# A spectral filter and a feed-forward on one core: W_in loaded in seven small pieces, the prologue rearranged around it, and stages B and Y a slot later

## Chip, core and metric

One core of one Trainium2 chip runs the whole program. The metric is the device time of one execution in microseconds (us). Each timed execution also lists its span (first to last instruction) and the mean clock that TensorE was granted. "Before" is the kernel as it stood, "changed" the kernel with the change.

## The reference, cut to what matters

```python
# x: (8, 3008, 256) f32; filt_r, filt_i: (1505, 256); w_in: (256, 2048); w_out: (2048, 256)
X = np.fft.rfft(x, axis=1)
y = np.fft.irfft(X * (filt_r + 1j * filt_i)[None], n=3008, axis=1)
h = np.maximum(y.reshape(24064, 256) @ w_in, 0.0)
out = (h * h) @ w_out
```

## The kernel before

The transform of length 3008 = 64 x 47 is done with matmuls, per batch: stage A (47 points) gives u, which goes through DRAM (dU) to be reordered; B (64 points), a product with the filter on VectorE, P back, giving ze, which goes through DRAM (dZ) and comes back as zt; stage Y gives yt, the input of the feed-forward. The feed-forward runs in 47 groups of 512 tokens, each group in 8 slots. In a slot TensorE does four matmuls of 512 columns (psH) and eight of 256 (psO, for the group before), and units of the next batch's stages are sprinkled into chosen slots. Batch 0's stages, and most of batch 1's stage A, form a prologue of some 50 us.

```python
    def load_win(k):                       # W_in, f32, in the same two buffers as x
        w32s[k] = p_x32.tile([128, DFF], F32, tag="x32", ...)
        nc.sync.dma_start(out=w32s[k], in_=moe_w_in[128 * k:128 * k + 128, :])
    ...
    def read_z(b, c, ks=(0, 1)):           # Z back from DRAM, two halves
        for k in ks:
            nc.sync.dma_start(out=zt[64 * k:64 * k + 48],
                              in_=v[48 * k:48 * k + 48, 8 * c:8 * c + 8, :])
    ...
    def fft_plan(b):                       # slot numbers, cut
        t0 = 14 if b == 1 else 18
        for p in range(12):
            r = t0 + (18 if b == 1 else 19) * p // 11
            put(r, 0, unit_b, b, p); put(r, 0, unit_s, b, p); put(r + 2, 1, unit_p, b, p)
        t0 = 35 if b == 1 else 40
        ... read_z at t0 ...
        for n in range(16):
            if b == 1:
                put(38 + n // 2 if n > 3 else 39, n % 2, unit_y, b, n)
            else:
                put(44 + n // 2, n % 2, unit_y, b, n)
    ...
    for k in range(7):                     # prologue: batch 0's B, product, P
        ... unit_b, place_f, unit_p0 ...
        if k in (1, 2):                    # here two of the three x tiles of batch 1 are loaded
            load_wide(1, k - 1)
            cast_wide(1, k - 1, nc.gpsimd, nc.gpsimd)
    read_z(0, 0); load_wout(0); read_z(0, 1); load_wout(1)
    for c in (0, 2, 1):
        chunk_a(1, c)                      # batch 1's stage A, three of four chunks
    for c in (0, 2, 1):
        write_u(1, c)
    for n in range(4):
        unit_y(0, n)                       # then the feed-forward starts
```

## Time and profile before

| what | value |
|---|---|
| timed executions, median (3) | 794.77 us (794.66 to 795.65) |
| the profiled execution's own time | 797.61 us, span 795.8 |
| its mean granted clock | 0.996 |
| TensorE / VectorE / ScalarE busy | 98% / 69% / 70% |
| first feed-forward matmul | 52.5 us from the span's start |

The execution that was profiled took 2.84 us longer than the timed median. The profile is read in the prediction.

### The profile page before, as it was taken

The numbers are of one execution on the slowest core, as the hardware profiler recorded it, in microseconds if no ns is written. First come the engines' busy times: TensorE is split into PE (matmuls) and PEld (weight loads), VectorE is DVE, ScalarE is ACT, GpSimd is POOL, SyncE is SP. The second block draws the span as 40 slices with busy tenths as digits, with TensorE's granted clock in tenths as the row PEclk, the third lists the DMA queues.
The fourth block names the chain that finished last, engine by engine and source line by source line (L and its number), as shares of the span: only waits on it lengthen the run. The fifth ranks groups of instructions, "written<-read, shape, count | busy, mean of one in ns | idle before, by whom it ended". The sixth has DMA issues, their size and how long they took to land.

```text
span 795.8 us, 14801 instructions
## 1 busy us (share of the span) xinstructions
PE 783.1 (98%) x6102; PEld 553.7 (70%) x6102; DVE 552.2 (69%) x898; ACT 554.9 (70%) x708; POOL 24.4 (3%) x27
## 2 busy tenths in 40 slices
PE   8989999999999999999999999999999999999998
PEld 5846677667676676867778676776777667776666
DVE  6946995579855897559965699557985589554342
ACT  3856776767777677767777677676776767766664
POOL 3710000000000000000000000000000000000000
PEclk9989999999999999999999999999999999999999
DMA  9994555336724467055471555525563342511111
GB/s 352 361 277 134 130 151 139 92 126 165 202 58 107 158 165 181 30 164 151 124 183 49 171 153 137 129 71 156 156 170 97 87 142 80 123 48 41 40 41 54
DMA packets 88139, 107.32 MB, mean 135 GB/s; under 512 B 6288, under 2 KB 78864, under 8 KB 83856
## 3 DMA queue, kind: packets, MB, share of 16 engines
q1 hardware_dynamic: 87864, 106.19, 46.9%
q8 instruction: 48, 0.79, 0.4%
q10 hardware_dynamic: 144, 0.18, 0.1%
q14 instruction: 19, 0.16, 0.1%
q0 software_dynamic: 64, 0.00, 0.0%
HBM read 58.12 MB, written 48.23 MB: 134 GB/s over the span
## 4 chain that ended last, share of the span: by engine, by line
PE 93%; DMA 3%; ACT 1%; DVE 1%; issue 0%; POOL 0%; SPq 0%; ACTq 0%; DVEq 0%; POOLq 0%
PE psO L577 40%; PE psH L560 39%; PE psA L359 3%; PE psY L530 3%; PE psB L443 2%; PE psP L494 2%; PE warm L274 1%; DMA ut<-dU 1%; DMA xw<-in_x_dram 1%; PE psf L293 1%; DMA dZ<-ze 1%; ACT h L564 1%; PE psf L296 0%; DMA dU<-u 0%; PE psA L380 0%; ACT sF L303 0%
## 5 line engine op out<-in xcount | busy, mean ns | idle before, releaser
L564 ACT ACTIVATE h<-psH 128x1024 f16<-128x1024 f32 x376 | 385.2, 1025 | 189.7 <-PE psH L560 188.2
L577 PE MATMUL psO<-sWout,h 128*128 128x256 f16 x3008 | 388.6, 272 | 0.0
L560 PE MATMUL psH<-yt,sWin 128*128 128x512 f16 (+7 forms) x1728 | 386.9, 351 | 1.7 <-DVE yt L539 0.8
L577 PEld LDWEIGHTS <-h 128*128 128x128 f16 x3008 | 290.6, 98 | 77.3
L568 DVE TENSOR_TENSOR h<-h 128x1024 f16<-128x1024 f16 x376 | 253.7, 685 | 100.8 <-ACT h L564 99.2
L560 PEld LDWEIGHTS <-sWin 128*128 128x128 f16 x1728 | 159.5, 98 | 101.7 <-issue 3.5
L451 DVE TENSOR_TENSOR prod<-psB,sF 128x1024 f16<-128x1024 f32 x84 | 102.4, 1219 | 5.9 <-PE psB L443 5.6
L539 DVE CAST yt<-psY 128x376 f16<-128x376 f32 x62 | 33.9, 549 | 57.4 <-PE psY L530 57.4
L365 DVE CAST u<-psA 96x512 f16<-96x512 f32 x50 | 34.3, 687 | 47.3 <-PE psA L359 45.1
L496 ACT CAST ze<-psP 128x512 f16<-128x512 f32 x84 | 49.2, 586 | 17.8 <-PE psP L494 15.9
L588 ACT COPY ost<-psO 128x512 f32<-128x512 f32 (+1 forms) x96 | 55.7, 580 | 6.7 <-PE psO L577 5.3
L530 PEld LDWEIGHTS <-zt 112*128 112x128 f16 x512 | 34.9, 98 | 12.1 <-issue 2.0
L530 PE MATMUL psY<-sC,zt 112*128 112x94 f16 x512 | 42.3, 205 | 0.6 <-DMA zt<-dZ 0.3
L465 DVE TENSOR_TENSOR yf<-prod,yf 128x512 f16<-128x512 f16 x84 | 35.7, 425 | 2.9
L443 PE MATMUL psB<-ut,sSB 128*128 128x256 f16 x192 | 36.5, 272 | 0.6 <-DMA ut<-dU 0.5
L359 PE MATMUL psA<-x,sC 94*96 94x512 f16 x96 | 36.6, 382 | 0.0
L443 PEld LDWEIGHTS <-sSB 128*128 128x128 f16 x192 | 18.6, 98 | 20.9 <-issue 1.7
L494 PE MATMUL psP<-yf,sSP 128*128 128x256 f16 x168 | 32.1, 273 | 0.2 <-ACT yt L537 0.2
L537 ACT CAST yt<-psY 128x376 f16<-128x376 f32 x66 | 30.7, 468 | 1.1 <-PE psY L530 0.6
L338 DVE CAST x<-x 94x2048 f16<-94x2048 f32 x24 | 29.2, 1216 | 0.0
L363 ACT CAST u<-psA 96x512 f16<-96x512 f32 x50 | 28.6, 572 | 0.0
L458 DVE COPY yf<-prod 64x512 f16<-64x512 f16 x84 | 24.3, 289 | 2.9
(63 smaller groups left out, 255.9 us busy)
## 6 DMA issues: line engine op xcount, KB each, us to landing
x<-in_x_dram SPq DMA_DIRECT2D x20, 768.0 KB
zt<-dZ SPq DMA_DIRECT2D x64, 192.0 KB
dU<-u SPq DMA_DIRECT2D x28, 384.0 KB
dZ<-ze SPq DMA_DIRECT2D x28, 384.0 KB
out_dram<-ost SPq DMA_DIRECT2D x66, 128.0 KB
out_dram<-ost SPq DMA_DIRECT2D x31, 256.0 KB
ut<-dU SPq DMA_DIRECT2D x7, 1024.0 KB
xw<-in_x_dram SPq DMA_DIRECT2D x4, 1024.0 KB
```

Source lines behind the costliest of these rows:

```text
L359: nc.tensor.matmul(ps[0:96, :], sSA, x16s[(b, c)][:, m, :], start=True, stop=True)
L443: nc.tensor.matmul(ps[:, i * D:(i + 1) * D], sSB[:, 2 * p + i, :], uts[b][:, 2 * p + i, :], start=True, stop=True)
L451: nc.vector.tensor_mul(out=prod, in0=ps.rearrange("p (a d) -> p a d", d=D).unsqueeze(1).to_broadcast([128, 2, 2, D]), in1=sF[:, :, 2 * p:2 ...
L465: nc.vector.tensor_add(out=yf, in0=prod[:, 0], in1=yf)
L494: nc.tensor.matmul(ps[:, i * D:(i + 1) * D], sSP[:, 2 * p + i, :], yf[:, i, :], start=True, stop=True)
L496: nc.scalar.copy(out=zes[(b, c)][:, 2 * i6:2 * i6 + 2, :], in_=ps.rearrange("p (a d) -> p a d", d=D))
L530: nc.tensor.matmul(ps[:, 94 * jj:94 * jj + 94], zt[:, 4 * (g % 2) + jj, dt * 128:(dt + 1) * 128], sSY, start=True, stop=True)
L560: nc.tensor.matmul(ps[:, i, o:o + n], sWin[:, dt, jt * 128:(jt + 1) * 128], yts[b][:, dt, r:r + n], start=(dt == 0), stop=(dt == 1))
L564: nc.scalar.activation(out=h2[:, 2 * s:2 * s + 2, :], in_=ps, func=AF.Relu)
L568: nc.vector.tensor_mul(out=v, in0=v, in1=v)
L577: nc.tensor.matmul(pso[g][:, t % 2, :], h2s[g][:, jt, t * 128:(t + 1) * 128], sWout[:, jt, :], start=(jt == 0), stop=(jt == NJT - 1))
L588: nc.scalar.copy(out=ost[:, h0:h0 + step, :], in_=pso[g][:, h0:h0 + step, :])
```

## The change

Its intent is to get all of x of batch 1 in early (so far one of its three tiles was, the other two waited for W_in's buffers): W_in no longer uses the x buffers but seven pieces in buffers that the main loop needs later. Around that, the filter's casts and evictions are spread differently over the engines. In the main loop B and Y of batches 2 to 7 come one slot later (more time for ut and zt to land), and batch 1's four Y units in one slot are spread out, for which its B is squeezed into one slot less. Cut to its core:

```diff
-    def load_win(k):
-        w32s[k] = p_x32.tile([128, DFF], F32, tag="x32", name=f"win32_{k}")
+        for k, c, n, pool, tag in ((0, 0, 768, p_ze, "ze"), (0, 768, 768, p_ze, "ze"),
+                                   (0, 1536, 512, p_prod, "prod"), ... 7 pieces ...):
+            nc.sync.dma_start(out=t, in_=moe_w_in[128 * k:128 * k + 128, c:c + n])
 ...
-        t0 = 14 if b == 1 else 18
+        t0 = 14 if b == 1 else 19
-            r = t0 + (18 if b == 1 else 19) * p // 11
+            r = t0 + (17 if b == 1 else 18) * p // 11
-        t0 = 35 if b == 1 else 40
+        t0 = 34 if b == 1 else 40
-                put(38 + n // 2 if n > 3 else 39, n % 2, unit_y, b, n)     # b == 1
-                put(44 + n // 2, n % 2, unit_y, b, n)                      # b > 1
+            put((38 if b == 1 else 45) + n // 2, n % 2, unit_y, b, n)
 ...
+    load_win()
+    for k in range(3):
+        load_wide(1, k)                    # x of batch 1, right behind W_in
 ...                                       # filter casts, place_f order: cut
-        if k in (1, 2):
-            load_wide(1, k - 1)
-            cast_wide(1, k - 1, nc.gpsimd, nc.gpsimd)
+    cast_wide(1, 2, nc.vector, nc.scalar)
```

More of the change, by code (lines that the diff above doesn't have):

```diff
@@ L210 @@
     xw32, xw16 = {}, {}
-    halves, later = ((0, 0), (0, 1)), []
     def load_wide(b, k):
@@ L218, in load_wide, with cast, cast_wide @@
         t = pool.tile([128, 8, D], F32, tag=tag, name=f"xw_{b}_{k}")
-        v = (v0[:, 0:8, :], v1, v0[:, 8:16, :])[k]
-        for m in (slice(0, 4), slice(4, 8)) if (b, k) in halves else (slice(0, 8),):
-            if m.stop > 4 and m.start == 4:
-                later.append((t, v, m))
-            else:
-                nc.sync.dma_start(out=t[:, m, :], in_=v[:, m, :])
-        xw32[(b, k)] = t
-    def cast_wide(b, k, *engs, parts=(0, 1)):
-        if 0 in parts:
-            xw16[(b, k)] = p_x16.tile([128, 8, D], F16, tag="x16", name=f"xw16_{b}_{k}")
-        for i in parts:
+        nc.sync.dma_start(out=t, in_=(v0[:, 0:8, :], v1, v0[:, 8:16, :])[k])
+        xw32[(b, k)] = t
+    def cast(eng, out, in_):
+        (eng.copy if eng is nc.scalar else eng.tensor_copy)(out=out, in_=in_)
+    def cast_wide(b, k, *engs):
+        t = p_x16.tile([128, 8, D], F16, tag="x16", name=f"xw16_{b}_{k}")
+        for i in range(2):
             m = slice(4 * i, 4 * i + 4)
-            engs[i].tensor_copy(out=xw16[(b, k)][:, m, :], in_=xw32[(b, k)][:, m, :])
-    for k in range(2):
+            cast(engs[i], t[:, m, :], xw32[(b, k)][:, m, :])
+        xw16[(b, k)] = t
+    for k in range(3):
         load_wide(0, k)
-    for t, v, m in later:
-        nc.sync.dma_start(out=t[:, m, :], in_=v[:, m, :])
-    load_wide(0, 2)
     f32s = []
@@ L276, with place_f @@
     f16s = []
-    def place_f(im, k, eng, rotate=False):
+    def place_f(im, k, *engs, rotate=False):
         if rotate:
@@ L299, in place_f @@
             n = t.shape[1]
+            eng = engs[i % len(engs)]
             dst = sF[:, im, 4 * k + 2 * i:4 * k + 2 * i + 2 * n, :]
@@ L311, with load_win, cast_win @@
     w32s = {}
-    def load_win(k):
-        w32s[k] = p_x32.tile([128, DFF], F32, tag="x32", name=f"win32_{k}")
-        nc.sync.dma_start(out=w32s[k], in_=moe_w_in[128 * k:128 * k + 128, :])
-    def cast_win(k):
-        for j in range(2):
-            c = slice(1024 * j, 1024 * j + 1024)
-            nc.gpsimd.tensor_copy(out=sWin[:, k, c], in_=w32s[k][:, c])
+    def load_win():
+        for k, c, n, pool, tag in ((0, 0, 768, p_ze, "ze"), (0, 768, 768, p_ze, "ze"),
+                                   (0, 1536, 512, p_prod, "prod"), (1, 0, 768, p_ze, "ze"),
+                                   (1, 768, 512, p_prod, "prod"), (1, 1280, 512, p_prod, "prod"),
+                                   (1, 1792, 256, p_yf, "yf")):
+            t = pool.tile([128, n], F32, tag=tag, name=f"win32_{k}_{c}")
+            nc.sync.dma_start(out=t, in_=moe_w_in[128 * k:128 * k + 128, c:c + n])
+            wins.append((t, k, slice(c, c + n)))
+    def cast_win():
+        for t, k, c in wins:
+            nc.gpsimd.tensor_copy(out=sWin[:, k, c], in_=t)
+    wins = []
     def load_wout(k):
@@ L390, in chunk_a, with chunk_a0 @@
                     eng.tensor_copy(out=o, in_=pv)
-    def chunk_a0(c, ks):
-        for k in ks:
+    def chunk_a0(c):
+        for k in range(2):
             banks, groups = bank_pair(f"psA_0_{c}_{k}")
@@ L641, in fft_plan @@
         for n in range(16):
-            if b == 1:
-                put(38 + n // 2 if n > 3 else 39, n % 2, unit_y, b, n)
-            else:
-                put(44 + n // 2, n % 2, unit_y, b, n)
+            put((38 if b == 1 else 45) + n // 2, n % 2, unit_y, b, n)
         return plan
@@ L653 @@
     uT = p_h2.tile([128, 2, NC, 128], F16, tag="h2", name="uT")
-    for i in range(2):
-        for k in range(2):
-            cast_wide(0, k, nc.vector, nc.vector, parts=(i,))
-    cast_wide(0, 2, nc.vector, nc.gpsimd)
+    for k in range(3):
+        cast_wide(0, k, nc.vector, nc.gpsimd if k == 2 else nc.vector)
     def load_const(t, d, k):
@@ L666 @@
         load_const(sSP[:, c, :], dSP, k)
-    for k in range(2):
-        load_win(k)
-    for k in range(2):
-        for c in (0, 2):
-            chunk_a0(c, (k,))
-    for k in range(2):
-        for c in (1, 3):
-            chunk_a0(c, (k,))
+    load_win()
+    for k in range(3):
+        load_wide(1, k)
+    for c in (0, 2, 1, 3):
+        chunk_a0(c)
     f16s.append(p_h2.tile([128, 2, QF + D], F16, tag="h2", name="f16"))
@@ L678 @@
         nc.gpsimd.tensor_copy(out=f16s[0][:, im, QF:], in_=nyq[:, im, :])
-    for im, e in ((0, e0), (0, e1), (1, e0)):
-        nc.gpsimd.tensor_copy(out=f16s[0][:, im, e], in_=f32s[im][:, e])
-    for k in range(2):
-        sSPx.append(p_u.tile([128, 12, 128], F16, tag="u", name=f"sSPx_{k}"))
-        c = slice(12 * k, 12 * k + 12)
-        nc.gpsimd.tensor_copy(out=sSPx[k][0:64], in_=sSP[64:128, c, :])
-        nc.gpsimd.tensor_copy(out=sSPx[k][64:128], in_=sSP[0:64, c, :])
-    for k in range(2):
-        cast_win(k)
-    uts[0] = p_ut.tile([128, NC, D], F16, tag="ut", name="ut_0")
-    load_wide(1, 2)
-    cast_wide(1, 2, nc.gpsimd, nc.gpsimd)
-    for k in range(6):
-        turn_u(k, nc.vector if k in (1, 3, 4, 5) else nc.scalar)
-        if k > 2:
-            place_f(0, k - 3, nc.scalar, True)
-    nc.vector.tensor_copy(out=f16s[0][:, 1, e1], in_=f32s[1][:, e1])
-    place_f(0, 3, nc.vector, True)
-    place_f(1, 0, nc.scalar)
+    for e in (e0, e1):
+        nc.gpsimd.tensor_copy(out=f16s[0][:, 0, e], in_=f32s[0][:, e])
+    uts[0] = p_ut.tile([128, NC, D], F16, tag="ut", name="ut_0")
+    turn_u(0, nc.scalar)
+    turn_u(1, nc.vector)
+    turn_u(2, nc.scalar)
+    turn_u(3, nc.vector)
+    place_f(0, 0, nc.scalar, rotate=True)
+    for eng, e in ((nc.vector, slice(0, 1024)), (nc.gpsimd, slice(1024, 2048)),
+                   (nc.scalar, slice(2048, QF))):
+        cast(eng, f16s[0][:, 1, e], f32s[1][:, e])
+    turn_u(4, nc.vector)
+    place_f(0, 1, nc.scalar, rotate=True)
+    turn_u(5, nc.vector)
+    place_f(1, 0, nc.scalar, nc.vector, rotate=True)
+    for k in range(6):
+        if k % 3 == 0:
+            sSPx.append(p_u.tile([128, 12, 128], F16, tag="u", name=f"sSPx_{k}"))
+        c, o = slice(4 * k, 4 * k + 4), slice(4 * k % 12, 4 * k % 12 + 4)
+        nc.gpsimd.tensor_copy(out=sSPx[-1][0:64, o, :], in_=sSP[64:128, c, :])
+        nc.gpsimd.tensor_copy(out=sSPx[-1][64:128, o, :], in_=sSP[0:64, c, :])
+    cast_win()
+    for k in range(2):
+        cast_wide(1, k, nc.gpsimd, nc.gpsimd)
     for k in range(7):
@@ L705 @@
             unit_p0(k - 1)
-        if k < 2:
-            place_f(0, k + 4, nc.scalar)
-        if k in (1, 2):
-            load_wide(1, k - 1)
-            cast_wide(1, k - 1, nc.gpsimd, nc.gpsimd)
+        if k < 4:
+            place_f(0, k + 2, nc.scalar)
+    cast_wide(1, 2, nc.vector, nc.scalar)
     read_z(0, 0)
```

## The prediction

> **What bounds the kernel now.** I read the page first (busy shares, slices, chain), then each engine's busy time in stretches, then the waits of TensorE and of the DMA queue, and last the timeline of the stretch that the change rebuilds. The page and the stretches:
>
> ```profile
> PE 783.1 (98%) x6102; PEld 553.7 (70%) x6102; DVE 552.2 (69%) x898; ACT 554.9 (70%) x708; POOL 24.4 (3%) x27
> ...
> 24.80:40.70 15.90, 14.85 (x139) 12.56 (x137) 14.08 (x13) 13.70 (x13) 12.91 (x12) 1.00 0.91 340
> 40.70:52.50 11.80, 9.72 (x50) 5.19 (x48) 4.61 (x7) 5.20 (x8) 2.03 (x2) 0.71 0.87 235
> 52.50:63.00 10.50, 9.30 (x51) 4.22 (x51) 7.52 (x13) 8.40 (x10) 0.00 (x0) 1.00 0.96 273
> 63.00:126.00 63.00, 62.79 (x468) 43.62 (x466) 53.47 (x90) 45.22 (x59) 0.00 (x0) 1.00 0.54 147
> 126.00:132.00 6.00, 5.38 (x63) 4.04 (x61) 2.75 (x6) 4.03 (x7) 0.00 (x0) 1.00 0.78 196
> 132.00:796.00 664.00, 659.57 (x5098) 468.54 (x5095) 451.91 (x744) 468.25 (x596) 0.00 (x0) 1.00 0.42 116
> ```
>
> The columns of a stretch are its length, then busy time of PE, PEld, DVE, ACT, POOL, then clock, DMA share and GB/s. From 63 us on TensorE is full, so only its own gaps can be won there. I added up start-to-start distances of all matmuls less their columns at the full rate: after 60 us the gaps come to about 5 us in all, in few places. The loose stretch is 40.7 to 52.5: 9.7 of 11.8 us busy, and at a clock of 0.71. What happens in it, engine by engine:
>
> ```profile
> 38.71 1.01 ACT L482 CAST ze<-psP 128x1024 f16<-128x1024 f32 x1 [0.30 <-PE psP L480]
> 40.85 1.01 ACT L482 CAST ze<-psP 128x1024 f16<-128x1024 f32 x1 [1.13 <-PE psP L480]
> ...
> 41.64 2.03 POOL L232 CAST xw<-xw 128x1024 f16<-128x1024 f32 x2 [2.26 <-DMA xw<-in_x_dram]
> ...
> 40.65 0.38 PE L378 MATMUL psA<-xw,sC 128*96 128x512 f16 x1
> 42.74 0.58 PE L380 MATMUL psA<-xw,sC 120*96 120x512 f16 x1 [1.71 <-POOL xw L232]
> 43.12 0.63 PE L378 MATMUL psA<-xw,sC 128*96 128x512 f16 x1
> 43.54 0.63 PE L380 MATMUL psA<-xw,sC 120*96 120x512 f16 x1
> ```
>
> Batch 1's stage A has started when it waits for the cast of x, which waits for a load issued at 34.44 and landed at 41.5. That load came so late because its buffer held W_in, cast only at 29.9 to 33.9. The second cost is in the last two lines: matmuls of 512 columns start 0.42 us apart, where later ones stand 0.22 apart. The clock record has the half clock from 41.9 to 48.7 us. The DMA queue's waits name what comes next:
>
> ```profile
> SPq L483 <- ACT ze L482: 16.1, 6, 8.8
> ...
> SPq L512 <- DMA dZ<-ze: 3.8, 4, 2.0
> ```
>
> Batch 0's Z goes through DRAM. From the landing records: the last ze is evicted at 41.86, its write lands at 44.59, the read of zt that needs it is issued at 44.60 and lands at 47.79. Stage Y of batch 0 began at 50.65, so this round trip had 2.9 us of slack. It is the next bound. For the main loop, the waits of TensorE after 60 us:
>
> ```profile
> PE psH L560 <- DVE yt L539: 0.8, 2, 0.5
> PE psB L443 <- DMA ut<-dU: 0.5, 1, 0.5
> PE psY L530 <- DMA zt<-dZ: 0.3, 1, 0.3
> PE psY L530 <- ACT yt L537: 0.3, 1, 0.3
> ```
>
> **What the Trainium skill says.** "TensorE: Matmul & The Clock Gate", part 1 on the HAM clock gate: the array falls to half clock after an idle window of about 3.4 us, windows run freely, and it needs a busy window to return. The trace agrees: the half clock lasted 6.83 us, two such windows, after a window (38.4 to 41.9) in which I count 1.3 us of matmuls. The page states no share of busy time at which a window counts as idle; here 1.3 us of 3.41 was too little, and the window from 52.1 with some 2.0 us was enough. "DMA: Bandwidth & Descriptors", section on the anatomy of one DMA, gives a fixed cost of about 2 us and bytes at 436 GB/s (measured there on the GpSimd path). The trace: 256 KB of Z took 2.7 us from issue to landing, 192 KB of zt 3.2 us, and 1 MB loads on a full queue landed 2.5 us apart. "VectorE: DVE Perf Modes", section on the TRN2 errata, says small instructions each pay a fixed latency on VectorE and ScalarE; it does not speak of GpSimd, where the change cuts sSPx into three times as many copies.
>
> **The change part by part.**
> 1. First x loads whole instead of in halves. The halves were cast at 5.8, 8.4, 9.5; whole tiles should land at about 7, 9.5, 12 from the same bytes. The warm-up matmuls end at 10.9 anyway. Worth 0.
> 2. W_in into seven pieces in ze, prod and yf buffers. Bytes are the same 2.1 MB and land by about 30.5, as before. GpSimd casts them at 29.9 to 34, as before (4 x 1.04 us becomes 7 smaller ones, perhaps +0.2). But the x buffers are free from the start: x of batch 1 is queued right behind W_in and lands at about 33.1, 35.6, 38.1 (2.5 us each). GpSimd casts the first two (2 x 2.03 us) from 34.1 to 38.2. Stage A needs them at 40.7: no wait. The third is cast by DVE and ACT after the loop (0.7 and about 1 us) and is needed only by the third chunk.
> 3. Stage A then is 24 x 0.217 = 5.2 us, 40.7 to 45.9, instead of ending at 50.65. This removes 1.9 us of wait and 14 x 0.21 = 2.9 us of half clock, 4.8 us in all.
> 4. The filter's imaginary part is cast by three engines at its landing (21.3) instead of half by GpSimd and the rest by DVE at 23.1. DVE's 1024 columns take 0.7, GpSimd's 1.04, ACT's about 0.95: done at 22.4. ACT then evicts place_f(0,1), 2 x 0.58 us, and place_f(1,0), 1.1 us, to 24.6. (By my count of the bank pairs, the latter falls on a single two-bank tile, so the second engine it names is not used.) First prods at 24.65 instead of 26.19: 1.5 us earlier.
> 5. But place_f(0,2..5) now all lie in the loop on ACT: 15 evictions instead of 13 after place_f(1,0). In the old loop they follow each other every 1.1 us (28.49, 29.63, 30.73, 31.83). place_f(1,5) is the twelfth: 24.6 + 12 x 1.11 = 37.9. Then the last two prods, 2 x 1.17: 40.25, the last P matmuls, and ze at about 40.9, which is where it stood (40.85). Part 4 is spent on part 5: sum 0.
> 6. So Y of batch 0 starts when zt lands, about 41.9 + 2.6 + 3.1 = 47.6, instead of 50.65: **3.0 us won of the 4.8**; the other 1.8 us turn into TensorE idling between 45.9 and 47.6.
> 7. Slots: B and Y of batches 2 to 7 a slot later give ut and zt about 2 us more. Gaps that I counted there: 0.13 at 166, 0.15 at 216, 0.67 at 261, 0.23 at 357, 0.47 at 597, sum 1.65. Batch 1: four Y units in one slot cost 0.43 + 0.21 + 0.47 = 1.1 us at 126.7 to 128.7; two a slot should free most. Against that, its B is squeezed into 17 slots where DVE is full (15.50 of 16 us busy from 76 to 92), and its zt is needed a slot earlier: I take back 0.7 us. Net **2.0 us**.
>
> Sum: 794.8 - 3.0 - 2.0 = 789.8. Nothing follows behind the main loop that could hide it, since TensorE is full to the end.
>
> **Rivals.**
> - *The half clock returns in a new place.* The idle 1.7 us before Y leaves about half of one window busy (0.6 us of A, some 1.1 of Y), between the 1.3 us that throttled and the 2.0 us that did not. If it throttles, some 4 slots of the first feed-forward group run 4 x 0.43 instead of ACT's 1.05 us pace: +2.5 us, about 792.3. I give it 0.35, which adds 0.9 in the mean. Against it: TensorE comes out of 5 dense microseconds.
> - *ACT is the bound of the prologue loop.* It was busy 13.70 of 15.90 us and gets two more evictions in it. If its pace is 1.2 rather than 1.11, ze ends 1 us later and so does Y: 791 without the throttle, 793 with it. If buffers let ACT run at its bare 1.05, ze comes 0.3 earlier.
> - *The Z trip is shorter than I think*, since no x load shares the queue any more: Y at 46.6, 789 or, with a full clock and all slot gaps gone, 788.
> - *Batch 1's denser B stalls TensorE through DVE*: the 2.0 us of part 7 shrink to 0.5. For it: DVE had to do some 39 us of work in a 36.5 us stretch by my sum already. Against: only one gap, 0.38 us at 83, came of it.
>
> **Range and chances.** 789.8 plus 0.9 for the throttle's chance gives 790.8 (rounded up). The ends are the third rival (788.2) and throttle plus slow ACT (793.6). Two per cent would be 15.9 us, more than the about 14 us of gaps after the warm-up, so faster by over 2% is nearly out; slower needs a stall of a size that no part suggests.
>
> **What would show it.** Right: no wait of stage A for x, its matmuls 0.22 apart; x of batch 1 landed before 39; first Y matmul between 46.5 and 48 after a wait for zt; last ze at about 41 with ACT nearly gapless before it; no pair of gaps near 126; no psB wait for ut in batches 2 to 7. Wrong: stage A still at half clock or waiting (GpSimd late), a clock below 1 in the stretch after Y starts, last ze past 42.5, new gaps between 75 and 115 where psP or psB waits for DVE, or seven small W_in loads that hold up the queue so that x lands after 40.

## The result, and the profile after

| | before | changed |
|---|---|---|
| median of the timed executions (4 each) | 795.21 us (794.66 to 796.75) | 793.79 us (793.20 to 794.09) |
| ratio of fast runs | 1 | 0.9978, 95% interval 0.9961 to 0.9995 |

A ratio is the mean time of one kernel's fast runs over that of the other's of the same rounds, so it isn't quite the ratio of the medians. The gain is some 1.4 to 1.8 us: within 2%, but above the range that was predicted (788.2 to 793.6).

The profile seems at first to say that the prediction was right. Its span went from 795.8 to 791.9 us, 3.9 us, where 4.0 were forecast (5.0 before the allowance for the throttle). The page's line and two stretches of the changed kernel (length, then busy PE, PEld, DVE, ACT, POOL, clock, DMA share, GB/s):

```profile
PE 778.9 (98%) x6102; PEld 552.5 (70%) x6102; DVE 550.3 (69%) x897; ACT 557.4 (70%) x711; POOL 23.6 (3%) x36
...
40.70:49.70 9.00, 7.02 (x52) 4.29 (x50) 4.79 (x7) 5.94 (x9) 0.00 (x0) 1.00 0.73 202
49.70:63.00 13.30, 12.11 (x68) 5.98 (x68) 9.48 (x17) 9.89 (x12) 0.00 (x0) 1.00 0.96 270
```

The clock is full throughout, and the timeline of TensorE in the prologue's end went as forecast:

```profile
40.87 0.38 PE L380 MATMUL psA<-xw,sC 128*96 128x512 f16 x1
41.09 0.38 PE L382 MATMUL psA<-xw,sC 120*96 120x512 f16 x1
...
46.56 0.27 PE L530 MATMUL psY<-zero 128*128 128x128 f16 x2 [0.29 <-ACT u L390]
48.26 0.33 PE L532 MATMUL psY<-sC,zt 112*128 112x94 f16 x4 [1.42 <-DMA zt<-dZ]
...
49.71 2.03 PE L562 MATMUL psH<-yt,sWin 128*128 128x512 f16 x8 [0.28 <-ACT yt L539]
```

Stage A no longer waits, its matmuls stand 0.22 us apart, and Y then waits 1.4 us for the read of Z. The feed-forward starts at 49.7 instead of 52.5, 2.8 us earlier. By the psO matmuls of each slot, that lead is 2.83 us at slot 8, 2.33 at slot 50 (batch 1 lost 0.5) and 4.03 at the end (batches 2 to 7 won 1.7).

The waits of TensorE after 60 us are now

```profile
PE psH L562 <- DVE yt L541: 0.7, 2, 0.5
PE psO L579 <- DVE h L570: 0.6, 1, 0.6
PE psP L496 <- DVE prod L453: 0.3, 1, 0.3
PE psP L496 <- ACT yt L539: 0.2, 1, 0.2
```

The waits for ut and zt are gone, as intended, and two waits for VectorE have come, both in batch 1.

So two numbers disagree: the traces differ by 4 us, the timed medians by 1.4. The changed kernel's profiled execution took 793.69 us, like its timed ones (793.2 to 794.1). The profile of before is the one that stands outside.

### The profile page after: what moved, and what is told of

The parts are those of the page before. It is cut to its first block, busy times and chain, and to the rows that moved or that the text cites. A ratio compares the mean times of both kernels' runs of the same rounds, so it can differ in the third digit from the quotient of the medians.

```text
span 791.9 us, 14822 instructions
## 1 busy us (share of the span) xinstructions
PE 778.9 (98%) x6102; PEld 552.5 (70%) x6102; DVE 550.3 (69%) x897; ACT 557.4 (70%) x711; POOL 23.6 (3%) x36
## 3 DMA queue, kind: packets, MB, share of 16 engines
q1 hardware_dynamic: 88296, 106.19, 46.5%
## 4 chain that ended last, share of the span: by engine, by line
PE 89%; DVE 6%; DMA 3%; ACT 1%; SPq 0%; issue 0%; DVEq 0%; ACTq 0%
PE psO L579 40%; PE psH L562 38%; PE psA L361 3%; PE psY L532 2%; PE psB L445 2%; DMA f<-in_filt_i_dram 2%; PE psP L496 2%; DVE prod L453 2%; DVE h L570 1%; DMA wout<-in_moe_w_out_dram 1%; PE psf L287 1%; PE psf L290 1%; DVE yf L467 0%; ACT sF L298 0%; DVE yf L461 0%; ACT h L566 0%
## 5 line engine op out<-in xcount | busy, mean ns | idle before, releaser
L566 ACT ACTIVATE h<-psH 128x1024 f16<-128x1024 f32 x376 | 384.9, 1024 | 189.3 <-PE psH L562 186.7
L498 ACT CAST ze<-psP 128x512 f16<-128x512 f32 x84 | 49.1, 585 | 17.2 <-PE psP L496 14.7
L532 PEld LDWEIGHTS <-zt 112*128 112x128 f16 x512 | 35.1, 98 | 11.6 <-issue 1.6
```

The costliest lines, as they stand in the source:

```text
L498: nc.scalar.copy(out=zes[(b, c)][:, 2 * i6:2 * i6 + 2, :], in_=ps.rearrange("p (a d) -> p a d", d=D))
L532: nc.tensor.matmul(ps[:, 94 * jj:94 * jj + 94], zt[:, 4 * (g % 2) + jj, dt * 128:(dt + 1) * 128], sSY, start=True, stop=True)
L566: nc.scalar.activation(out=h2[:, 2 * s:2 * s + 2, :], in_=ps, func=AF.Relu)
```

## The experiments

Theory 1: the half clock in stage A belongs to the execution that was profiled, not to the kernel; at the full clock the Z trip already bound the prologue, so that the changed prologue moves nothing and the whole gain comes from the slots. Theory 2, the rival: the half clock is in every execution of before, the profiler only adds a constant, and the prologue's 2.8 us are real.

The kernels were run in three groups of four, each group on one chip with its own runs of before. "Full" below means a mean clock of 0.999 or 1.000 (the half clock at the very end is after the work), lower values mean that one or more windows ran at half clock.

### The kernel before, unchanged

No edit.

> The kernel before, unchanged, to see the clock of every execution. Theory 1 (the profile that the prediction read was an odd execution: its own time was 797.61 us against a timed median of 794.77, and its half clock in stage A cost 14 x 0.21 = 2.9 us that most executions don't pay): most executions at a mean clock of 0.999 or more and a span near 793.0 us, and any execution with a clock near 0.996 some 2.9 us longer. Theory 2 (the half clock is in every execution, and the profiler only adds a constant): all executions near 0.996, with no link of clock and span.

Five rounds: 797.33 us against 796.68 of its twin, ratio 1.0007 (0.9988 to 1.0027). What counts is the clock. Over all groups there are 41 executions of before with their clock on record:

| mean clock | executions | mean us | range |
|---|---|---|---|
| 0.999, 1.000 | 19 | 795.80 | 794.77 to 798.34 |
| 0.997, 0.998 (one window at half) | 15 | 797.04 | 796.08 to 798.16 |
| 0.995, 0.996 (two windows) | 7 | 798.73 | 798.23 to 799.81 |

The half clock comes in 22 of 41 and costs 1.2 us for one window and 2.9 for two, in the means. Theory 2 falls: the profiled execution had the rarest and dearest state, two windows. Theory 1 was off in two points: the full executions are 19 of 41 and not "most", and it named a span of 793.0, while the full ones spread over 3.6 us, so the clock is not the only thing that varies.

### Two more looks at the kernel before

No edit; one profile each.

> The kernel before once more, for a trace of an execution at the full clock (about half of them are). Theory 1, if the clock is full: stage A's matmuls 0.22 us apart, its end near 47.8, first Y matmul near 48.0, first feed-forward matmul near 49.7, which is where the changed kernel's stands (49.4 to 49.7); so the prologue's change is worth nothing in such an execution. Theory 2: even at the full clock the changed prologue is ahead by 1.5 us or more. If the clock is at half for one window (0.998), first feed-forward matmul near 51.2.

> A second trace of the kernel before, for the same purpose and with the same expectation as the look ahead of it.

The first look took 797.39 us at a clock of 0.997, the second 795.12 at 0.999. Their stretches of nine microseconds, the first look's first:

```profile
40.70:49.70 9.00, 6.73 (x24) 3.46 (x24) 2.81 (x4) 4.01 (x6) 2.02 (x2) 0.81 0.80 227
```

```profile
40.70:49.70 9.00, 6.86 (x49) 4.13 (x48) 4.59 (x7) 5.09 (x8) 2.02 (x2) 1.00 0.82 237
```

The bracketed counts show how much further the second look is at 49.70. In both, 23 of the matmuls that start in the stretch are stage A's; at full clock 25 small ones of Y follow, with one half window none of them has begun. The second look's timeline of TensorE, to be held against the changed kernel's above:

```profile
42.65 0.38 PE L380 MATMUL psA<-xw,sC 120*96 120x512 f16 x1 [1.76 <-POOL xw L232]
42.87 0.38 PE L378 MATMUL psA<-xw,sC 128*96 128x512 f16 x1
...
47.78 0.28 PE L528 MATMUL psY<-zero 128*128 128x128 f16 x2
47.89 0.33 PE L530 MATMUL psY<-sC,zt 112*128 112x94 f16 x4
...
49.64 2.07 PE L560 MATMUL psH<-yt,sWin 128*128 128x512 f16 x8 [0.25 <-ACT yt L537]
```

Stage A still waits 1.8 us for x. But it ends at 47.8, and by the landing records zt lands at 47.74, so Y starts without a wait. The feed-forward starts at 49.64, against 49.71 in the changed kernel. One pair of traces would not be enough, as the read of zt takes longer in some executions than in others. But over all traces at full clock the feed-forward starts at 49.19 and 49.64 with the old prologue (no filler), and between 49.14 and 49.71 with the new one (four traces). **At the full clock the new prologue is worth nothing that these traces can tell**: it turns a wait for x into an about equally long wait for zt.

Why one execution throttles and another doesn't can be worked out from the traces: the clock record changes on a grid of 3.413 us, and the grid's offset differs from run to run. Summing the columns of all matmuls in each window (at the rate of its clock) gives, for the emptiest window near the wait:

| trace (all with the old prologue) | emptiest window | TensorE work in it | what followed |
|---|---|---|---|
| before, first look | 39.87 to 43.29 | 0.92 us | one window at half |
| before, as profiled | 38.46 to 41.87 | 1.11 us | two windows at half |
| before with all of the changed slots | 39.97 to 43.39 | 1.14 us | one window at half |
| before, unchanged | 40.57 to 43.99 | 1.16 us | one window at half |
| before, second look | 38.16 to 41.57 | 1.27 us | nothing |
| before with batches 2 to 7 moved | 39.58 to 42.99 | 1.36 us | nothing |

Up to 1.16 us of work in a window (34%) the clock fell, from 1.27 us (37%) on it didn't. These are few windows, and a matmul record missing from a trace would shift a figure. For the return, 2.60 us of work at half clock were not enough (the profiled execution, hence its second window), 3.30 us were; in the warm-up of the trace with batches 2 to 7 moved, 2.8 us were.

### The kernel before with the wait filled

```diff
+    pw = psO("fill").rearrange("p a d -> p (a d)")
+    for _ in range(8):
+        nc.tensor.matmul(pw, zero, sF[:, 0, 0:2, :], start=True, stop=True)
     for c in (0, 2, 1):
         chunk_a(1, c)
```

> The kernel before with eight matmuls of zero weights (512 columns, 8 x 0.22 us) put ahead of batch 1's stage A, in the 1.9 us in which TensorE waits for x, so that no window is idle. Theory 1: all executions at the full clock, stage A at 0.22 us a matmul, first Y matmul about 48.0 when zt lands, median unchanged (794.3 to 795.0), no execution above 796. Theory 2: the half clock goes in every execution, so the median falls by up to 2.9 us to about 792.

All six executions had the full clock, and the trace's first feed-forward matmul came at 49.71 us. The filler alone, with x still late, brings the trace where the changed prologue brings it. The median was 796.52 us, ratio 1.0001 (0.9981 to 1.0022): theory 2's 2.8 us are not there. Theory 1's absolute figures missed (it allowed no execution over 796, five of six were). One reason can be read in the trace: in batch 2 it waits 1.4 us for zt, a wait of the old slots that was 0.15 us in the first profile. Its slowest execution, 799.11 us, had a clock of 1.000 too; why it was slow stays open. The removal of a half clock that is in half of the executions ought to show as about 1 us in the mean; the interval is too wide to see that.

### The changed prologue alone

The changed kernel with `fft_plan` of before.

> The kernel before with the changed prologue alone (W_in in seven pieces, early x of batch 1, casts), its old slots kept. Theory 1: with the clock full, the wait of stage A for x was hidden behind the trip of Z through DRAM, so the median stays within 0.5 us of before (about 794.8), only never at the half clock. Theory 2: 2.8 us faster, about 792.0.

796.57 us, ratio 0.9998 (0.9980 to 1.0016), all six at full clock. The trace's feed-forward starts at 49.1, and yet nothing is left in the time. So the prologue, the larger half of the change and of the forecast, gives nothing that five rounds can resolve; the 3.0 us that were forecast for it would be a ratio of 0.9962, outside the interval. Against the full executions of before (19 of them, 795.80) its six are 0.7 us slower in the mean (796.49). I can't settle whether that is more than scatter (the groups ran on different chips); its trace has one long wait for ut, 1.5 us at 639 us, of the kind that the old slots have at random.

### The changed slots alone

Before with `fft_plan` of the changed kernel.

> The kernel before with the changed slots alone. From the two traces, the difference after the prologue grew from -2.83 to -4.03 us, so both theories expect about 1.2 us faster than before at the same clock, near 793.6: 1.7 us won in batches 2 to 7 and 0.5 us lost in batch 1. Theory 1 says that this is all of the change's gain; theory 2 that it is less than half of it.

794.91 us, ratio 0.9978 (0.9957 to 0.9998), the same ratio as the whole change, although four of six executions ran one window at half clock. At the full clock it took 794.17 us (two executions) against 795.64 of before in that group, 1.5 us less where 1.2 were expected. Both theories had expected such a gain; theory 1 that it is all, with which the two runs together agree, within intervals of about 1.5 us to either side.

### Batches 2 to 7 alone

```diff
-        t0 = 14 if b == 1 else 18
+        t0 = 14 if b == 1 else 19
-            r = t0 + (18 if b == 1 else 19) * p // 11
+            r = t0 + 18 * p // 11
-                put(44 + n // 2, n % 2, unit_y, b, n)
+                put(45 + n // 2, n % 2, unit_y, b, n)
```

> The kernel before with stages B and Y of batches 2 to 7 one slot later, batch 1's slots and the prologue as they were. The old slots' waits for ut and zt in batches 2 to 7 sum to 1.65 to 3.4 us in the four traces that have them, none in the traces with the new ones: so 1.7 to 3 us faster than before at the same clock, and half a microsecond or so better than all of the changed slots.

794.50 us, ratio 0.9964 (0.9944 to 0.9984). At the full clock 792.6 (two executions) against 795.7 of before (three in that group), about 3 us, at the upper end of what was expected; few executions, so I take the sign and not the size. The waits of its TensorE after 60 us are down to

```profile
PE psH L560 <- DVE yt L539: 0.3, 1, 0.3
PE psY L530 <- ACT yt L537: 0.3, 1, 0.3
PE psP L494 <- ACT yt L537: 0.2, 1, 0.2
```

that is, to those of batch 1's old slots. These few slot numbers do at least as much as the whole change.

### The changed kernel with batch 1's old slots

```diff
-            r = t0 + (17 if b == 1 else 18) * p // 11
+            r = t0 + 18 * p // 11
-        t0 = 34 if b == 1 else 40
+        t0 = 35 if b == 1 else 40
-            put((38 if b == 1 else 45) + n // 2, n % 2, unit_y, b, n)
+            put((38 + n // 2 if n > 3 else 39) if b == 1 else 45 + n // 2, n % 2, unit_y, b, n)
```

> The changed kernel with the old slots of batch 1 alone (B over 18 slots, four Y units in slot 39), those of batches 2 to 7 as changed. From the two traces batch 1's new slots cost 0.5 us net (gaps of 0.44, 0.75 and 0.35 us came, 1.1 us went): so about 0.5 us faster than the changed kernel, with the gap near 124 to 126 back. If the four Y units were the cost, as the prediction had it, 0.4 us or more slower.

792.97 us, ratio 0.9964; at the full clock 793.0 against 793.5 of the changed kernel in the same group, and its lead over that kernel's trace grew by 0.5 us through batch 1. The stretches show the trade. Changed kernel:

```profile
108.00:114.00 6.00, 5.57 (x40) 3.61 (x37) 5.87 (x11) 4.38 (x6) 0.00 (x0) 1.00 0.75 199
114.00:120.00 6.00, 5.84 (x41) 4.02 (x42) 4.87 (x7) 3.96 (x5) 0.00 (x0) 1.00 0.56 160
```

With batch 1's old slots:

```profile
108.00:114.00 6.00, 6.00 (x45) 4.23 (x44) 5.84 (x11) 4.34 (x6) 0.00 (x0) 1.00 0.75 184
120.00:126.00 6.00, 5.38 (x49) 3.51 (x47) 2.89 (x5) 3.52 (x6) 0.00 (x0) 1.00 1.03 201
```

In both, VectorE (third busy figure) is full from 108 to 114. With 17 slots TensorE has to wait for it there (5.57 of 6.00); with 18 it doesn't, and pays instead at 123 to 126 for four Y units in a slot. The new gaps are 0.44, 0.75 and 0.35 us, the old ones 1.11 in sum.

### The changed kernel once more

No edit.

> The changed kernel, unchanged, as the control of this chip, with the clock of every execution. All executions at a clock of 0.999 or more; about 0.2 per cent faster than before over all executions. Theory 1 (the change's prologue gains only what the half clock cost, and its slots the rest): against those executions of before that had the full clock the gain is about 1.2 us, against those at 0.998 or less 2.5 to 4 us.

794.77 us, ratio 0.9978 (0.9965 to 0.9991). The expectation that it never throttles was wrong: three of five executions had 0.998, and took 794.95 us in the mean against 793.50 of the other two. So the new idle stretch ahead of Y most likely does to the clock, in some executions, what the old one ahead of stage A did. No throttled execution of the changed kernel was traced, so the place is inferred: in its first trace a window of the grid, wherever it might lie between the warm-up and the end of the work, holds 2.1 us of work or more, except around Y's wait, where the emptiest position (from 46.1) holds 1.05 us. Against the full executions of before in that group (795.63) the full ones gain 2.1 us, more than the 1.2 expected, with two executions.

Its own trace has Y's wait again, a little shorter than in the first:

```profile
47.94 0.33 PE L532 MATMUL psY<-sC,zt 112*128 112x94 f16 x4 [1.11 <-DMA zt<-dZ]
...
49.39 2.03 PE L562 MATMUL psH<-yt,sWin 128*128 128x512 f16 x8 [0.28 <-ACT yt L539]
```

### A shorter trip for Z, with a wrong result

```diff
         for k in ks:
+            j = 0 if (b, c) == (0, 0) else k
             nc.sync.dma_start(out=zt[64 * k:64 * k + 48],
-                              in_=v[48 * k:48 * k + 48, 8 * c:8 * c + 8, :])
+                              in_=v[48 * j:48 * j + 48, 8 * c:8 * c + 8, :])
```

The first tile of Z is read twice from its earlier half, so the result is wrong (relative error 0.21); only the wait is of interest.

> The changed kernel with a wrong result on purpose: the first tile of batch 0's Z is read twice from its first half, which is written some 3 us earlier than the second, so stage Y of batch 0 waits less for the trip through DRAM. Theory 1 with the Z trip as the bound of the new prologue: first Y matmul at about 46.6 instead of 48.2, first feed-forward matmul about 48.1 instead of 49.7, and 1.5 us off the total. Rival (Y is held by the end of stage A and the evictions of its banks): no change, within 0.3 us.

TensorE's timeline:

```profile
46.65 0.27 PE L531 MATMUL psY<-zero 128*128 128x128 f16 x2 [0.29 <-ACT u L390]
47.47 0.33 PE L533 MATMUL psY<-sC,zt 112*128 112x94 f16 x4 [0.54 <-DMA zt<-dZ]
...
48.92 1.39 PE L563 MATMUL psH<-yt,sWin 128*128 128x512 f16 x5 [0.28 <-ACT yt L540]
```

Against the control of its group, above, the wait for zt shrank from 1.11 to 0.54 us and the feed-forward moved up by 0.47 us, from 49.39 to 48.92, not by the 1.5 to 1.6 expected. The second read was issued 1.5 us earlier (43.16 against 44.62) but took 4.2 us instead of 3.2; why, was not tested. The time at full clock, 793.18 us (five executions) against 793.50 (two), differs by 0.3 us, which the rival allows for, so the times alone decide nothing. What speaks for the Z trip as the bound is the traces' order: zt landed at 48.12, 47.80 and 47.33 us in the changed kernel, its control and this run, and Y's first matmul on it started 0.14 us later each time, while the zero matmuls ahead of it, which need stage A's end and a bank, were ready by 46.65.

### Work put into the wait

The fourth chunk of batch 1's stage A is moved from the main loop into the prologue, where TensorE waits for Z anyway:

```diff
-        u = p_u.tile([96, 8, D], F16, tag="u", name=f"u_{b}_{c}")
+        pool, tag = (p_x16, "x16") if c == 3 else (p_u, "u")
+        u = pool.tile([96, 8, D], F16, tag=tag, name=f"u_{b}_{c}")
-        for a in range(12 if b == 1 else 0, 16):
+        for a in range(16 if b == 1 else 0, 16):
-    for c in (0, 2, 1):
+    for c in (0, 2, 1, 3):
         chunk_a(1, c)
-    for c in (0, 2, 1):
+    for c in (0, 2, 1, 3):
         write_u(1, c)
```

> The changed kernel with batch 1's fourth chunk of stage A moved into the prologue's wait, its B left in the changed slots: separates the two parts of the version that was 2.1 us faster. Theory 1: 1 to 1.7 us faster than the changed kernel at the full clock (about 792), no execution at the half clock, since TensorE's idle stretch before Y is gone; the gaps of batch 1 (0.44, 0.75, 0.35) stay. Rival: the chunk only delays the feed-forward, no gain over the changed kernel (793.5).

791.98 us, ratio 0.9935 (0.9918 to 0.9952), all six executions at full clock and within 0.43 us of one another. The changed kernel did not run in this group; in the group before, its full executions took 793.50 us, with the full ones of before at 795.63 there and 795.71 here. The feed-forward starts at 49.79, so the chunk did find its room.

With u of batch 1 written that early, its B can also begin two slots sooner and take 20 slots instead of 18:

```diff
-        put(10 if b == 1 else 14, 1, read_u, b)
-        t0 = 14 if b == 1 else 19
-            r = t0 + (17 if b == 1 else 18) * p // 11
+        put(7 if b == 1 else 14, 1, read_u, b)
+        t0 = 12 if b == 1 else 19
+            r = t0 + (19 if b == 1 else 18) * p // 11
```

> The changed kernel with stage A's fourth chunk of batch 1 moved from the main loop into the prologue, into TensorE's wait for the Z trip (8 matmuls of 0.22 us, 1.74 us), and batch 1's B begun two slots earlier, over 20 slots. Theory 1 with the Z trip as the bound: the 1.7 us of work are free there, first feed-forward matmul stays near 49.7 (at most 0.5 later), and VectorE's gaps of batch 1 (1.5 us) shrink: 1.5 to 3 us faster than the changed kernel. Rival (the prologue is full): the feed-forward starts 1.7 us later and only the gaps of batch 1 are won, under 1 us.

791.28 us (791.12 to 791.73), ratio 0.9940 (0.9929 to 0.9952), correct, all five at full clock. Against the changed kernel of the same group it gains 3.0 us in the mean, of which 2.1 at the same clock and the rest because it never throttles. Its timeline shows the filled wait:

```profile
47.71 0.38 PE L383 MATMUL psA<-xw,sC 120*96 120x512 f16 x1
47.93 0.28 PE L531 MATMUL psY<-zero 128*128 128x128 f16 x2
48.28 0.33 PE L533 MATMUL psY<-sC,zt 112*128 112x94 f16 x4
...
49.93 1.24 PE L563 MATMUL psH<-yt,sWin 128*128 128x512 f16 x5 [0.48 <-ACT yt L540]
```

Stage A now ends where Z arrives; with eight more matmuls the feed-forward starts at 49.93, 0.2 and 0.5 us later than in the two traces of the changed kernel. The spread of B brings 0.35 us over the version without it, by the traces (the two ran in different groups). This is the version that beats both kernels, and the changed prologue leaves the room for it: there stage A ends at 46.1, 1.8 to 2.1 us before Y's first matmul on zt, while in the old one at full clock it ends at 47.8, when zt has landed, so that a fourth chunk would have no wait to fill. That is read from the traces; the old prologue with a fourth chunk was not run.

## Why the prediction was wrong

**The step that failed is the sum of parts 3 and 6: "This removes 1.9 us of wait and 14 x 0.21 = 2.9 us of half clock" and "3.0 us won of the 4.8".** The 2.9 us of half clock were read from an execution of 797.61 us and subtracted from a median of 794.77. That execution had two windows at half clock, as 7 of 41 do; 19 of 41 have none. At the full clock stage A ended at 47.8, not 50.65, and so the "2.9 us of slack" that the prediction gave the Z trip was not slack: it was the half clock itself, seen from the other side. The term measured 0.0 us at full clock, within the scatter of the traces (the feed-forward's start at 49.19 and 49.64 before, 49.14 to 49.71 with the new prologue), and the prologue alone gave a ratio of 0.9998. Over the mix of states one would expect about 1 us of it back; that stayed below what the runs resolve.

**Parts 1, 2, 4 and 5 held.** The first x tiles landed whole at 6.6, 9.1 and 11.6 us (forecast 7, 9.5, 12). x of batch 1 landed at 32.4, 34.9 and 37.4 us (forecast 33.1, 35.6, 38.1). The first product began at 24.4 (24.65), the last ze at 41.07 (40.9), the same place as before: ScalarE's two extra evictions did eat what the earlier start had won. One term inside part 4 was off: VectorE's cast of 1024 columns took 1.51 us beside GpSimd's, not 0.7 (0.69 in the same kernel's other casts of that size); the filter's landing at 20.4 instead of 21.3 made up for it. Y's matmul came at 48.26, after a wait for zt as the check list had it, but 0.3 us past the window of 46.5 to 48 that it gave.

**Part 7 was right for batches 2 to 7 and had the wrong sign for batch 1.** The waits for ut and zt (1.65 us in the first profile, 1.9 to 3.4 in the other traces with the old slots) went altogether: from the first feed-forward matmul to the last matmul of the feed-forward, before with these slots moved is 2.1 us shorter than the second look, both at full clock. Batch 1 was booked at +0.4 us net (1.1 won, 0.7 taken back) and came out at -0.5: the new gaps sum to 1.54 us and not 0.7. Net, the slots are all of the gain that the runs resolve.

**The rivals.** "The half clock returns in a new place" was given 0.35. It was not in any of the four executions, but in three of five of the second set, at 1.45 us each. The mechanism was right as far as the traces tell (the place is inferred); what the prediction did not ask is whether the half clock was always in the *old* place. Its two marks were misread as well: by columns the window that throttled held 1.11 us, not 1.3, and the one from 52.1 held 2.36, not 2.0. "Batch 1's denser B stalls TensorE through DVE" was right too. The other two did not come: the last ze was not late, and the read of zt took 3.5 us, no less than the 3.2 before.

The view that would have caught it was on the table: a profiled time 2.84 us above the timed median and 1.96 above the slowest timed run, and a mean clock of 0.996, which is just what 6.83 us at half clock make of 796 (1 - 3.41 / 796 = 0.9957).

## What to carry to other kernels

Before a wait is priced from a profile, hold the profiled execution's own time and clock against the timed runs; what most executions don't show (here two windows at half clock, in 7 of 41) is not there to be won from the median. When a wait is removed, look for the wait that ends next and compute its place in the state that most runs have. And an idle stretch that can't be shortened is best filled with work that is needed anyway: it takes that work off the full main loop and keeps the clock up.

## What the Trainium skill lacked or had wrong

- "TensorE: Matmul & The Clock Gate", part 1: it says that the clock falls after an idle window of about 3.4 us and that the windows run freely. The traces agree on the grid (3.413 us) and on the free phase, but an "idle" window needn't be idle: it fell with 0.92 to 1.16 us of matmul work in the window, and not with 1.27 us or more, and 2.60 us at half clock did not bring it back where 2.8 and 3.30 did. The page gives no such share.
- The same section puts the ramp penalty at less than 1% of a kernel and advises against fitting a count of cold matmuls, which it says varies from run to run. Here it is 0.15% (1.2 us) or 0.36% (2.9 us) of the time, but that is as large as the change under test, and it makes one kernel's executions two or three populations. No page says to look at the clock of each timed execution.
- "DMA: Bandwidth & Descriptors", anatomy of one DMA: the fit of 2.0 us plus bytes at 436 GB/s gives 2.6 us for 256 KB of Z and 2.45 for 192 KB of zt (both are estimates from the page, which measured another path). The last write of Z took 2.4 us in the changed kernel, which agrees; the read of zt behind it took 3.5 us (3.2 in the control), with other transfers in the queue.
- "GPSIMD Engine Reference", section 3.1, names the two dispatch hops of a GpSimd instruction without a figure; section 2.1 gives tens of cycles for one of them, the call in the wrapper, and no total per instruction. Here copies of 64 x 1536 (f16) took 1.46 to 1.59 us and of 64 x 512 0.61 us, so three short ones cost about 0.3 us more than one long one.
